# S5 input products of a token pair summed in one PSUM bank, with the first half copied out midway, under a new order of work

## Chip, cores and metric

The kernel runs on one core of one Trainium2 chip. The metric is the device time of one execution in microseconds; three runs of the kernel before give a median of 349.37 us (349.33 to 352.1). Inputs are bfloat16, with 2048 tokens of 640 channels. TensorE (PE) multiplies 128x128 tiles into PSUM, which has 8 banks of 512 float32 columns here; ScalarE (ACT) and VectorE (DVE) copy from PSUM to SBUF and do the element-wise work; GpSimd (POOL) does little; SyncE (SP) issues most of the DMA.

## What is computed

Two kinds of layers alternate twice: x = x + A(LN(x)), x = x + B(LN(x)), and again with the same weights. A is a diagonal complex state space model (S5), B a gated long convolution (H3). Cut to what matters here:

```python
def _A_ref(x, Lambda_re, Lambda_im, B_re, B_im, C_re, C_im, log_dt, Dskip):
    Lam_bar = jnp.exp(dt * Lam)
    B_bar = ((Lam_bar - 1.0) / Lam)[:, None] * Bmat
    Bu = jnp.einsum("bld,pd->blp", x + 0j, B_bar)
    for t in range(L):
        h = Lam_bar[None, :] * h + Bu[:, t, :]
        hs.append(h)
    y = 2.0 * jnp.einsum("blp,dp->bld", hseq, Cmat).real + x * Dskip[None, None, :]

x = x + _A_ref(_layernorm(x, axis=-1), ...)
x = x + _B_ref(_layernorm(x, axis=-1), ...)
x = x + _A_ref(_layernorm(x, axis=-1), ...)
x = x + _B_ref(_layernorm(x, axis=-1), ...)
```

The gate and the filter of B do not depend on x, so the kernel computes the convolution once and uses it in both B layers.

## The kernel before

**Tasks in a written order.** The kernel is a list of 909 named tasks, each on one engine. The string `ORDER` names them in the order in which they are emitted, so each engine runs its own tasks in that order; a suffix `/a`, `/d` or `/p` puts a task that could run on two engines on ACT, DVE or POOL. All SBUF data lies in one tile `arena` and all PSUM data in one tile `banks`; the table `PLACE` gives each buffer its offset in the arena and each PSUM buffer its first bank. Two buffers may share a place at different times, and semaphores then make the later one wait. `Sched.run` does nothing but walk the order.

**The tasks of the set-up and of the convolution.** `yt_*` make Fourier tables, `kv_*` the shifted and gated k and v, `a_*` the S5 weights in four forms (`BT0`, `BT1` for the input, `W0`, `W1` for the output) and the turning table. `yq0` to `yq4` are five blocks of 128 channels of the convolution: products `KA`, `KB`, `VA`, `VB`, `IB`, `IA` on PE, each group `:m` with its copy from PSUM `:e` on ACT or DVE (`evac`, L254 for ACT and L256 for DVE), a pointwise product `_pw` on DVE (L1175 to L1178), a transposition `_tt` and a store `_st` by DMA. Almost all of this is done in the first 160 us.

**The S5 layers.** `A1` and `A2` each run over four chunks `c0` to `c3` of 512 tokens (`ALayer.chunk`). Tokens are taken in pairs, an earlier and a later one, so a chunk has 256 pairs, and the recurrence runs over pairs with the square of the eigenvalue. The steps of a chunk, with their tasks:

- layer norm: statistics `_ln_bn` (first layer, L582 and L583 on DVE) or `_ln_sq` (L555 on ACT), then `_sd`, `_post`, and the normalisation `_id:0` to `:3` on ACT (L609) or DVE (L611);
- `_tu`: a DMA transposition of the normalised chunk, issued by SP (L639);
- the input products in three groups of output blocks j = (0, 1), (2, 3), (4). `_bq` multiplies the second half of `uT` by `BT0` (L658), `_eq` copies the result to the SBUF buffer `q`, `_bp` multiplies the first half of `uT` by `BT1` (L673) and adds `q` by a product with the identity matrix (L675), and `_ev` copies the sum into the buffer `g`. Each j has two parts (real and imaginary) of 256 columns, one bank in all; `_bq` has its banks `pq`, `_bp` its banks `pb`;
- on DVE: `_ri`, a turn of `g` (L690, L691, after a memset L694), `_sc`, the scan (L707), `_cy`, the carry to the next chunk, `_ro`, the turn back, and `_hx`, the subtraction of `q` from the state (L732);
- `_cp:0` to `:3`: the output products with the skip term, 128 tokens each (L755, in the first layer 27 matmuls, of which two add the residual by the identity), and `_xe:0` to `:3`, the copy out (L763 on ACT, L765 or L767 on DVE).

**The B layers.** `B1` and `B2` take the layer norm of the new x (`_ln_*`, `_u`), multiply by the stored convolution (`_mm`, L812) and add (`_m`, L818 and L820). The convolution is loaded from DRAM by `B1l*` and `B2l*`, the output stored by `_st`.

**What the change touches.** The loop over the three groups in `ALayer.chunk`, `ORDER` and `PLACE`. Weights, layer norm, turns, scan, output products, B layers and convolution keep their code.

Of the kernel before, what the change touches and what calls it, by code (L numbers as in the profile page):

```python
# [54 lines left out]
    warm yt_io6 kv_kd a_ldB1 a_pl kv_pd1/p kv_pd3/p kv_pd2/p yt_io0 yt_ph6 yt_f0 kv_dsl yt_ph0 yt_sin6 a_ldB0 yt_io12 kv_pd0/p yt_f2 yq0_kl yt_ph12  # L55
    yt_sin0 a_p0 kv_d0 a_b01:3 kv_k0 kv_lk0 a_b00:2 a_b0e1:3/d kv_k1 a_b00:3 a_b0e0:2/d kv_d1 yt_f3 a_b0e0:3/a kv_k2 a_p1 yt_f4 a_b00:4 yt_sin12 a_p2
    a_b01:2 kv_lv0 yt_neg6 a_ti a_b01:4 yt_h0 yq0_ka a_b0e1:2/d kv_d2 a_b0e1:4/d yq0_KA:m2 kv_ds0 yq0_KA:m3 a_b0e0:4/a yq0_KA:e2/d yq0_KA:m1 a_p3 yq1_kl
    yq0_KA:m0 kv_ds1 yt_neg12 kv_mm0:0 yt_neg0 yq0_KA:e1/a yq0_KA:e0/d kv_ds2 yq0_KA:e3/a a_p4a kv_lv1 a_p4 a_b00:1 a_p5a yq0_KB:m1 a_b0e0:1/a kv_ds3
    kv_ev0:0 a_ta kv_mm0:1 yq0_KB:e1/d kv_ds4 yq0_KB:m4 kv_lk1 a_b00:0 yq1_ka kv_ev0:1 a_p5b yq0_KB:m0 yt_h1 a_b0e0:0/d yq0_KB:m2 yq0_vl yq0_KB:e4/a a_t0
    yq0_KB:e0/a a_b01:0 a_b01:1 yq0_KB:e2/a a_b0e1:1/a a_p6 a_ldC0 a_t1 a_b0e1:0/d kv_mm1:1 a_lamd kv_mm1:0 a_ldC1 kv_ev1:1 a_b10:1 kv_ev1:0 yq0_VA:m2  # L60
    yq0_KB:m3 a_b1e0:1/d yt_Si yq0_VA:m3 yq0_VA:e2/a yq0_KB:e3/d yq1_KA:m1 yq0_VA:e3/a yq0_VA:m0 yq1_KA:e1/d a_b11:4 yq0_VA:e0/a yq0_VA:m1 yq1_KA:m2
    a_b1e1:4/a yq0_VA:e1/d a_b10:4 yt_Ci yq1_KA:e2/a yq1_KA:m3 yq0_VB:m3 a_b1e0:4/a yq1_KA:e3/d yt_h2 yq0_VB:m0 yq0_VB:e3/a yt_h3/p yq1_KA:m0 a_b10:0
    yq0_VB:e0/d yq1_KA:e0/a yq0_VB:m1 yq1_vl a_f a_b1e0:0/a a_ct1 yq0_VB:e1/a yq0_VB:m2 yt_nsi a_wc01:0 a_b11:0 kv_lk2 yq0_VB:m4 a_wm01:0 a_b1e1:0/a
    yq0_VB:e2/d a_wc01:1 a_b11:3 yq0_VB:e4/a xl0 a_wm01:1 a_b1e1:3/a yq1_KB:m2 yq0_pw yq1_KB:m3 yq1_KB:e2/a yq1_KB:m0 kv_lv2 yq1_KB:e3/a yq1_KB:m1
    yq1_KB:e0/a a_b10:2 a_b11:1 yq1_KB:e1/a a_b11:2 kv_lk3 a_b1e1:1/a a_b10:3 a_b1e1:2/a yq1_VA:m3 kv_pd4/p a_b1e0:3/a kv_mm2:1 yq1_VA:e3/a kv_lv3
    yq1_VA:m0 a_b1e0:2/a kv_ev2:1 yq0_IB:m3 yq1_VA:e0/a yq0_IB:m0 yq0_IB:e3/d kv_mm2:0 yq0_IB:e0/a yq2_kl yq1_VA:m2 yq0_IB:m1 kv_ev2:0 yq1_VA:e2/a
    yq0_IB:m4 yq0_IB:e1/a A1c0_ln_bn:2/d yq1_VA:m1 yq2_vl a_ct0 yq1_VA:e1/a yq0_IB:e4/d yq0_IB:m2 A1c0_ln_bn:0/d a_wc00:0 yq1_VB:m0 a_t2 yq1_KB:m4
    a_wm00:0 yq1_VB:e0/a yq0_IB:e2/d a_wc00:1 yq1_VB:m1 yq1_KB:e4/a A1c0_ln_bn:3/a a_wm00:1 yq0_tt kv_mm3:0 yq1_VB:e1/d a_ct4 kv_ev3:0 a_ct2 a_wc04:0
    a_wc02:0 a_wm04:0 yq1_VB:m3 a_wm02:0 a_wc04:1 a_wc02:1 a_wm04:1 yq1_VB:e3/a a_wm02:1 yq1_VB:m2 yq2_ka kv_lv4 yq2_KA:m3 yq2_KA:m0 yq1_VB:e2/d kv_mm3:1
    yq2_KA:e3/a yq2_KA:e0/a yq1_VB:m4 yq2_KA:m2 kv_ev3:1 a_dd yq1_VB:e4/a yq2_KA:e2/a yq2_KA:m1 kv_lk4 yq1_pw yq2_VA:m2 yq2_KA:e1/a yq2_VA:m3 yq2_VA:e2/a  # L70
    xl2 yq2_VA:e3/a yq2_VA:m0 yq2_KB:m0 yq2_VA:e0/a yq2_KB:m2 yq2_KB:e0/a a_ct3 yq2_KB:e2/a yq2_KB:m4 yq3_kl yq0_IA:m0 a_wc03:0 yq2_KB:m1 yq0_IA:e0/a
    a_wm03:0 yq2_KB:e1/a yq1_IB:m3 yq3_vl yq2_KB:e4/d a_wc03:1 A1c0_ln_bn:1/d yq1_IB:m4 kv_mm4:1 yq1_IB:e3/a a_wm03:1 yq1_IB:e4/a yq1_IB:m1 kv_ev4:1
    yq2_VA:m1 yq0_IA:m1 yq1_IB:e1/a yq2_VA:e1/d yq4_kl yq1_IB:m2 yq1_IB:m0 yq0_IA:e1/d yq1_IB:e2/a yq2_VB:m1 yq1_IB:e0/d A1c0_ln_sd kv_mm4:0 yq3_ka
    yq2_VB:e1/d yq1_tt yq2_VB:m0 kv_ev4:0 yq2_KB:m3 yq2_VB:e0/a yq2_VB:m2 A1c0_ln_post yq2_KB:e3/a A1c2_ln_bn:1/d yq2_VB:m3 yq2_VB:e2/a A1c0_id:3/d
    yq2_VB:m4 yq3_KA:m1 A1c0_id:2/d yq2_VB:e3/a yq2_VB:e4/d yq3_KA:m2 A1c0_id:0/d yq3_KA:m3 yq3_KA:e1/a A1c0_id:1/d yq3_KA:m0 yq2_pw A1c0_tu yq3_KA:e2/a
    yq3_VA:m2 yq3_KA:e3/a yq3_KA:e0/a yq1_IA:m0 yq3_VA:e2/a yq3_KB:m4 yq0_st yq1_IA:m1 yq1_IA:e0/a yq3_KB:m1 yq1_IA:e1/a yq3_KB:m3 xl1 yq3_KB:e1/a
    yq3_VA:m3 A1c0_bq:2 yq3_KB:e4/a yq3_KB:e3/a yq3_VA:e3/d yq2_IB:m2 yq1_st A1c0_eq:2/a A1c2_ln_bn:3/d yq2_IB:m4 yq2_IB:m3 yq2_IB:e2/a yq2_IB:e4/d
    yq2_IB:m1 A1c2_ln_bn:2/d yq2_IB:e3/a yq4_vl yq3_VA:m1 yq3_KB:m0 A1c1_ln_bn:2/d yq2_IB:e1/a yq2_IB:m0 yq3_VA:e1/a A1c1_ln_bn:1/d yq3_KB:m2 yq2_IB:e0/a
    A1c2_ln_bn:0/d A1c0_bp:2 yq3_KB:e2/a yq2_tt A1c1_ln_bn:3/d A1c2_ln_sd yq3_VA:m0 A1c0_bq:1 A1c0_ev:2/a A1c2_ln_post yq3_KB:e0/a A1c2_id:3/d yq4_ka
    A1c1_ln_bn:0/d yq3_VA:e0/a yq4_KA:m3 A1c2_id:1/d yq4_KA:m0 A1c0_eq:1/a yq3_VB:m2 yq4_KA:e3/d yq4_KA:e0/a yq3_VB:m1 A1c2_id:2/d A1c2_id:0/d A1c1_ln_sd  # L80
    yq3_VB:e2/a yq3_VB:m3 A1c2_tu yq3_VB:e1/d yq3_VB:m0 A1c1_ln_post yq3_VB:m4 A1c0_bp:1 yq3_VB:e0/a A1c1_id:2/d A1c1_id:0/d yq3_VB:e4/d yq3_VB:e3/a
    A1c1_id:3/d xl3 A1c1_id:1/a yq3_pw yq4_KA:m1 A1c0_bq:0 A1c0_ev:1/a A1c1_tu yq4_KA:e1/a yq4_KA:m2 A1c2_bq:2 A1c0_eq:0/a yq2_IA:m1 A1c0_bp:0 yq2_IA:e1/a
    yq4_KA:e2/a A1c2_eq:2/d yq2_IA:m0 A1c0_xr A1c0_ev:0/a yq3_IB:m1 yq2_IA:e0/a A1c2_bp:2 A1c0_ri yq3_IB:e1/a A1c1_bq:0 A1c2_ev:2/a yq4_KB:m2 yq3_IB:m3
    A1c0_sc yq4_KB:e2/a yq3_IB:m2 yq3_IB:e3/a yq4_KB:m3 A1c1_eq:0/a A1c1_bq:1 yq3_IB:e2/a yq4_KB:e3/a yq3_IB:m4 yq4_KB:m1 A1c1_eq:1/a yq3_IB:e4/d
    yq3_IB:m0 A1c3_ln_bn:1/a yq4_KB:e1/d A1c1_bq:2 A1c3_ln_bn:3/d A1c2_bq:0 yq3_IB:e0/a A1c0_cy A1c0_ro A1c1_eq:2/a yq3_tt yq4_KB:m4 yq4_KB:m0 A1c2_eq:0/a
    A1c1_bp:0 yq4_KB:e0/a yq4_KB:e4/d A1c1_bp:2 A1c3_ln_bn:2/d A1c1_ev:0/a yq4_VA:m2 yq4_VA:m0 yq2_st A1c1_ev:2/d A1c1_bp:1 yq4_VA:e0/a A1c3_ln_bn:0/d
    yq4_VA:e2/a yq4_VA:m1 yq4_VA:m3 A1c1_ev:1/d A1c2_bp:0 yq4_VA:e1/a A1c1_ri yq4_VA:e3/a A1c2_bq:1 A1c2_ev:0/a A1c3_ln_sd yq4_VB:m3 A1c2_eq:1/a A1c0_hx
    yq4_VB:m2 yq4_VB:e3/a yq3_IA:m1 A1c3_ln_post yq4_VB:m4 yq4_VB:e2/d A1c2_bp:1 yq3_IA:e1/a A1c1_sc yq4_VB:e4/a yq4_VB:m1 yq4_VB:m0 yq4_VB:e1/a A1c0_cp:3
    yq4_VB:e0/a A1c2_ev:1/a a_w10:3 A1c0_xe:3/d a_w11:0 a_w1e0:3/a a_w10:4 yq4_pw a_w1e1:0/a a_w10:1 a_w1e0:4/a a_w11:2 a_w1e0:1/a a_w10:0 a_w1e1:2/a
    a_w11:3 a_w10:2 A1c0_cp:1 a_w1e0:2/a a_w1e0:0/a a_w1e1:3/a a_w11:4 A1c0_xe:1/a yq3_IA:m0 A1c1_cy A1c1_xr a_w11:1 a_w1e1:4/a A1c1_ro yq4_IB:m1  # L90
    a_w1e1:1/a yq4_IB:m3 A1c3_id:3/a yq3_IA:e0/a A1c0_cp:0 yq4_IB:e1/a yq3_st yq4_IB:e3/a A1c1_hx yq4_IB:m2 A1c3_id:1/d A1c0_xe:0/a A1c3_id:2/d yq4_IB:m0
    A1c3_id:0/a yq4_IB:e2/d yq4_IB:m4 A1c0_cp:2 yq4_IB:e0/a A1c2_ri yq4_IB:e4/a yq4_tt A1c1_cp:3 A1c0_xe:2/a B1c0_ln_nm B1c0_ln_sq:1 A1c2_sc B1c0_ln_sq:0
    B1c0_ln_sq:3 A1c1_cp:0 A1c3_tu A1c1_xe:3/a yq4_IA:m1 A1c1_xe:0/a yq4_IA:m0 A1c2_xr A1c1_cp:2 A1c2_cy yq4_IA:e0/a yq4_IA:e1/d B1c0_ln_sq:2 yq4_st
    B1c0_ln_sd B1c0_ln_post A1c2_ro A1c1_cp:1 A1c1_xe:2/a B1c0_u:2/a A1c3_bq:1 B1l0 A1c1_xe:1/a B1c0_u:0/d B1c1_ln_nm B1c1_ln_sq:2 A1c2_hx A1c3_bq:0
    B1c1_ln_sq:3 B1l1 A1c3_eq:1/d B1c1_ln_sq:1 B1c0_u:3/d B1c1_ln_sq:0 A1c3_xr A1c2_cp:0 B1c0_u:1/d B1c0_mm B1c1_ln_sd A1c3_eq:0/a B2l0 B1c0_m:2
    B1c1_ln_post B1c0_m:0 B1c1_u:0/a A1c3_bq:2 B1c1_u:1/d A1c2_xe:0/a B1c0_m:1 A1c3_bp:1 B1c1_u:3/a B1c0_m:3 A1c3_eq:2/a B1c1_u:2/d A2c0_ln_nm
    A2c0_ln_sq:0 B1c1_mm A1c3_bp:2 A2c0_ln_sq:3 B1c1_m:1 A2c0_ln_sq:2 A1c3_bp:0 B1c1_m:2 A2c0_ln_sq:1 B1c1_m:0 A2c0_ln_sd A1c3_ev:1/a A2c0_ln_post
    A1c2_cp:1 A2c0_id:1/d A1c3_ev:2/a A2c0_id:2/d A1c3_ev:0/a B1c1_m:3 A2c0_id:0/a A1c3_ri A2c0_id:3/a A1c2_cp:3 A2c1_ln_nm A2c1_ln_sq:0 A2c0_tu
    A1c2_xe:1/a A2c1_ln_sq:1 A2c1_ln_sq:3 A1c2_cp:2 A1c3_sc B1l2 A2c1_ln_sq:2 A2c1_ln_sd A1c2_xe:3/a A2c0_bq:0 A1c2_xe:2/a B1c2_ln_nm B1c2_ln_sq:1
# [514 lines left out]
class ALayer:  # L614
# [6 lines left out]
    def chunk(self, c, src, sums_in, x_ready, resid, s_x, sums_out, s_src, reload):  # L621
# [26 lines left out]
        for gi, js in enumerate(((0, 1), (2, 3), (4,))):  # L648
# [3 lines left out]
            def e_bq(_, js=js, s_pq=s_pq):  # L652
                pq = s_pq.get().rearrange("p (j c n) -> p j c n", c=2, n=NB)
                uT, bt0 = s_uT.get(), w["BT0"].get()
                for jj, j in enumerate(js):
                    for c2 in range(2):
                        for k in range(NJ):
                            nc.tensor.matmul(pq[:, jj, c2, :], lhsT=bt0[:, c2, k, j * P:(j + 1) * P],  # L658
                                             rhs=uT[:, 2:4, k, :], start=(k == 0), stop=(k == NJ - 1))
# [721 lines left out]
```

## Time and profile before

| What | Value |
|---|---|
| Median of three runs | 349.37 us |
| Profiled execution, first to last instruction | 348.2 us |
| Granted TensorE clock, mean over the span | 0.977 |
| DVE: last instruction ends | 345.0 us |
| PE: last matmul ends | 331.7 us |
| Copy of 128x1024 from PSUM: ACT, DVE | 1.033 us, 1.220 us |
| Copy of 128x640 from PSUM: ACT, DVE | 0.720 us, 0.816 us |
| Copy of 128x512 from PSUM: ACT, DVE | 0.603 us, 0.689 us |
| Normalisation of 128x640: ACT; DVE from float32, from bfloat16 | 0.911 us; 0.608, 0.434 us |
| Turn on DVE: products, sum | 2.844 us, 1.504 us |
| Scan on DVE, one of two parts | 2.833 us |

The profile is one execution. Busy time of an engine is the time in which at least one of its instructions runs. Matmuls are pipelined: a row's mean duration of a matmul is its whole way through the array, and several are under way at once, so a busy PE is not a PE at its peak; the distance between the starts of two matmuls in a row is what one costs. An idle time is put down to what ended it. In the windows, the first number pair is the stretch of the span and its length, and after each engine's busy time stands the number of its instructions.

### The profile page before, as it was taken

To read this page: it belongs to the slowest core of one execution; us is meant where nothing else is said; L and a number is where in the kernel's file an instruction comes from. 1 tells how busy PE (TensorE), PEld (TensorE's weight loads), DVE (VectorE), ACT (ScalarE), POOL (GpSimd) and SP (SyncE) were. 2 spreads that over 40 slices of the span, in tenths; PEclk is the share of its full clock that TensorE was granted. 3 is DMA by queue.
4 is the path that set the end of the run, shared out by engine and by line. 5 is a ranking of instruction groups with operands and counts; after the bars stand their busy time and mean duration, and the time that the engine had idled before them with its cause. 6 is when DMAs were issued, how large, how long until landed. Compare 5 with 4: busy or idle time off the path is not lost.

```text
span 348.2 us, 9466 instructions
## 1 busy us (share of the span) xinstructions
PE 310.0 (89%) x4110; PEld 248.4 (71%) x4110; DVE 326.5 (94%) x449; ACT 256.3 (74%) x411; POOL 20.6 (6%) x62
## 2 busy tenths in 40 slices
PE   7777897779799999999999999999999999998910
PEld 7665887768698899896666786876877787654500
DVE  8999898899999989798999999999999999999996
ACT  6999898797998768566867689897776856008850
POOL 5690000010000000000000000000000000000000
PEclk9999999899999999999999999999999999999975
DMA  8999999887999920800259642315009500000024
GB/s 231 218 170 257 186 228 154 167 185 152 180 230 179 218 77 10 174 2 0 77 120 215 189 177 52 100 18 130 6 5 227 135 15 2 0 2 0 3 112 188
DMA packets 105868, 41.71 MB, mean 120 GB/s; under 512 B 98141, under 2 KB 100706, under 8 KB 105826
## 3 DMA queue, kind: packets, MB, share of 16 engines
q1 hardware_dynamic: 105680, 41.10, 53.7%
q8 instruction: 32, 0.52, 0.6%
q14 instruction: 10, 0.08, 0.1%
q10 hardware_dynamic: 146, 0.01, 0.0%
HBM read 19.02 MB, written 5.24 MB: 70 GB/s over the span
## 4 chain that ended last, share of the span: by engine, by line
PE 62%; DVE 27%; ACT 6%; issue 3%; POOL 0%; DVEq 0%; ACTq 0%; POOLq 0%
PE banks L755 18%; PE banks L658 11%; PE banks L673 11%; ACT arena L254 5%; DVE arena L256 3%; DVE arena L690 3%; DVE arena L707 3%; DVE arena L820 3%; DVE arena L767 3%; PE banks L1197 2%; PE banks L1198 2%; PE banks L675 2%; PE banks L1098 2%; PE banks L1289 2%; PE banks L1122 2%
## 5 line engine op out<-in xcount | busy, mean ns | idle before, releaser
L254 ACT ACTIVATE arena<-banks 128x1024 bf16<-128x1024 f32 (+4 forms) x150 | 129.5, 929 | 31.9 <-PE banks L658 9.2
L755 PE MATMUL banks<-arena 128*128 128x128 bf16 (+1 forms) x800 | 101.0, 283 | 1.7 <-DVE arena L767 1.7
L755 PEld LDWEIGHTS <-arena 128*128 128x128 bf16 x800 | 60.6, 98 | 41.7 <-issue 1.9
L673 PE MATMUL banks<-arena 128*128 128x256 bf16 x400 | 53.2, 273 | 0.0
L256 DVE CAST arena<-banks 128x1024 bf16<-128x1024 f32 (+4 forms) x43 | 41.7, 979 | 5.6 <-PE banks L675 2.5
L658 PE MATMUL banks<-arena 128*128 128x256 bf16 x400 | 46.2, 273 | 0.0
L690 DVE TENSOR_TENSOR arena<-arena 128x5160 bf16<-128x5160 bf16 x16 | 45.5, 2844 | 0.4
L707 DVE TENSOR_TENSOR_SCAN arena<-arena 128x1290 bf16<-128x1290 f32 x16 | 44.7, 2833 | 0.3
L673 PEld LDWEIGHTS <-arena 128*128 128x128 bf16 x400 | 38.6, 98 | 4.6
L658 PEld LDWEIGHTS <-arena 128*128 128x128 bf16 x400 | 38.5, 98 | 4.7
L555 ACT ACTIVATE junk<-arena,nmean 128x640 bf16<-128x640 f32 x48 | 39.7, 827 | 1.3
L1122 PE MATMUL banks<-arena 128*128 128x128 bf16 x170 | 35.5, 221 | 4.6 <-DVE arena L427 1.5
L1125 PE MATMUL banks<-arena 128*128 128x128 bf16 x170 | 35.7, 221 | 0.0
L1127 PE MATMUL banks<-arena 128*128 128x128 bf16 x150 | 33.2, 221 | 0.0
L1124 PE MATMUL banks<-arena 128*128 128x128 bf16 x150 | 33.2, 221 | 0.0
L609 ACT ACTIVATE arena<-arena,nmr,rstd 128x640 bf16<-128x640 f32 (+1 forms) x32 | 27.8, 912 | 5.8 <-DVE nmr L568 3.8
L691 DVE TENSOR_TENSOR arena<-arena 128x2580 bf16<-128x2580 bf16 x16 | 24.1, 1504 | 0.5
L675 PE MATMUL banks<-arena,ident_bf 128*128 128x256 bf16 x80 | 21.8, 273 | 0.0
L763 ACT ACTIVATE arena<-banks 128x640 f32<-128x640 f32 x15 | 10.4, 697 | 14.0 <-PE banks L755 14.0
L1197 PE MATMUL banks<-arena 128*128 128x128 bf16 x160 | 19.6, 219 | 0.7 <-ACT arena L254 0.5
L1198 PE MATMUL banks<-arena 128*128 128x128 bf16 x160 | 19.4, 219 | 0.3 <-DVE arena L1178 0.3
L1124 PEld LDWEIGHTS <-arena 128*128 128x128 bf16 x150 | 14.8, 99 | 5.1 <-issue 5.1
(196 smaller groups left out, 498.8 us busy)
## 6 DMA issues: line engine op xcount, KB each, us to landing
arena<-in_A_x_dram SPq DMA_DIRECT2D x8, 640.0 KB, 5.5
arena<-ysd SPq DMA_DIRECT2D x8, 640.0 KB, 5.9
arena<-in_B_ssm_k_dram SPq DMA_DIRECT2D x5, 512.0 KB, 7.7
arena<-in_B_v_dram SPq DMA_DIRECT2D x5, 512.0 KB, 6.3
ysd<-arena SPq DMA_DIRECT2D x5, 512.0 KB, 4.5
out_dram<-arena SPq DMA_DIRECT2D x8, 320.0 KB, 2.2
arena<-in_A_B_im_dram SPq DMA_DIRECT2D x1, 800.0 KB, 5.2
arena<-in_A_B_re_dram SPq DMA_DIRECT2D x1, 800.0 KB, 7.1
```

The lines of the kernel that those rows point to most:

```text
L254: nc.scalar.activation(out, in_, ACT.Copy)
L256: nc.vector.tensor_copy(out, in_)
L555: nc.scalar.activation(small.junk, src(q), ACT.Square, bias=st["nmean"][:, i:i + 1], scale=1.0, accum_out=st["ssq"][:, i:i + 1])
L658: nc.tensor.matmul(pq[:, jj, c2, :], lhsT=bt0[:, c2, k, j * P:(j + 1) * P], rhs=uT[:, 2:4, k, :], start=(k == 0), stop=(k == NJ - 1))
L673: nc.tensor.matmul(pb[:, jj, c2, :], lhsT=bt1[:, c2, j, k, :], rhs=uT[:, 0:2, k, :], start=(k == 0), stop=False)
L690: nc.vector.tensor_tensor(tt, gs[:, :, None].to_broadcast([P, 2, 2, n]), by_pairs(w["tab"].get().rearrange("p i j b -> p (i j b)"), n), AL ...
L707: nc.vector.tensor_tensor_scan(gv, rt, gv, 0.0, ALU.mult, ALU.add)
L755: nc.tensor.matmul(pc[:, o0:o1], lhsT=lh, rhs=rh, start=(n == 0), stop=(n == len(ops) - 1))
L1122: nc.tensor.matmul(ps[:, g, 0, :], lhsT=T["Cf"].get()[:, q, :], rhs=are, start=True, stop=single)
L1124: nc.tensor.matmul(ps[:, g, 0, :], lhsT=T["Sf"].get()[:, q, :], rhs=A[:, 2 * q + 1, :], start=False, stop=True)
L1125: nc.tensor.matmul(ps[:, g, 1, :], lhsT=T["NSf"].get()[:, q, :], rhs=are, start=True, stop=single)
L1127: nc.tensor.matmul(ps[:, g, 1, :], lhsT=T["Cf"].get()[:, q, :], rhs=A[:, 2 * q + 1, :], start=False, stop=True)
```

## The change

In each of the three groups the second product now adds into the bank of the first one. `_bq` starts the bank once (its very first matmul), `_eq` copies the bank's state out to `q`, and `_bp` then goes on adding into the same bank, without a start and without identity matmuls. `_ev` copies the sum. So `pq` is gone and `_bp` has 20 instead of 24 matmuls in a group of two blocks, 10 instead of 12 in the last. `q` is still needed by `_hx`. `skip_group_check` tells the language's checker that the group is read before its end.

```diff
-            s_pq, s_pb = S.bank(f"{nm}_pq{gi}", len(js)), S.bank(f"{nm}_pb{gi}", len(js))
-            n = len(js)
+            s_pb, n = S.bank(f"{nm}_pb{gi}", len(js)), len(js)
 
-            def e_bq(_, js=js, s_pq=s_pq):
-                pq = s_pq.get().rearrange("p (j c n) -> p j c n", c=2, n=NB)
+            def e_bq(_, js=js, s_pb=s_pb):
+                pb = s_pb.get().rearrange("p (j c n) -> p j c n", c=2, n=NB)
...
-                            nc.tensor.matmul(pq[:, jj, c2, :], lhsT=bt0[:, c2, k, j * P:(j + 1) * P],
-                                             rhs=uT[:, 2:4, k, :], start=(k == 0), stop=(k == NJ - 1))
+                            nc.tensor.matmul(pb[:, jj, c2, :], lhsT=bt0[:, c2, k, j * P:(j + 1) * P],
+                                             rhs=uT[:, 2:4, k, :], start=(c2 == k == 0), stop=(c2 == 1 and k == NJ - 1), skip_group_check=True)
...
                             nc.tensor.matmul(pb[:, jj, c2, :], lhsT=bt1[:, c2, j, k, :],
-                                             rhs=uT[:, 0:2, k, :], start=(k == 0), stop=False)
-                        nc.tensor.matmul(pb[:, jj, c2, :], lhsT=ident[:], rhs=s_q.get()[:, c2, j, :], start=False, stop=True)
+                                             rhs=uT[:, 0:2, k, :], start=False, stop=(c2 == 1 and k == NJ - 1), skip_group_check=True)
```

`ORDER` and `PLACE` are new from end to end. The 909 tasks are the same, in another order. 93 change their engine: 45 go from ACT to DVE, 43 from DVE to ACT, and five small ones from POOL to DVE. A part of the new order, around the first chunk's input products:

```
yq1_IA:e0/a A1c0_bq:2 yq3_KB:e2/a yq3_VA:m1 yq2_IB:m2 yq3_VA:e1/d yq1_st A1c0_eq:2/a
yq2_IB:m0 yq4_vl yq2_IB:e2/a A1c1_ln_bn:1/d yq2_IB:m1 yq2_IB:e0/a A1c1_ln_bn:0/d yq2_IB:e1/a yq2_IB:m3 yq4_KA:m2
yq0_st yq2_IB:e3/a a_dd yq4_KA:e2/d yq2_IB:m4 A1c0_bp:2 yq2_IB:e4/a yq3_VA:m2 yq3_VA:e2/d yq3_VA:m0 A1c0_bq:1 yq2_tt
yq3_VA:e0/a A1c2_ln_post A1c2_id:3/d A1c0_ev:2/a yq3_VB:m2 A1c2_id:0/d A1c0_eq:1/a A1c2_id:2/d A1c2_id:1/d yq3_VB:m4
yq3_VB:m3 A1c1_ln_bn:3/d yq3_VB:e4/a A1c1_ln_sd A1c0_bp:1 yq3_VB:e2/d A1c2_tu yq3_VB:e3/d A1c1_ln_post A1c1_id:0/d
A1c0_ev:1/a yq4_KA:m1 A1c1_id:1/d yq3_VB:m1 yq4_KA:e1/d yq3_VB:m0 A1c0_bq:0 yq3_VB:e1/a yq3_VB:e0/a A1c1_id:2/d
A1c1_id:3/d A1c1_tu yq3_pw A1c2_bq:2 A1c0_eq:0/a yq2_IA:m1 A1c0_bp:0 A1c2_eq:2/a yq2_IA:e1/a A1c2_bp:2 A1c0_ev:0/a
```

## The prediction

> **What bounds the kernel now.** I read the busy shares first, then the stretches of the span, then the chain that ended last, then the rows of the work that the change removes or moves. From the page:
>
> ```profile
> span 348.2 us, 9466 instructions
> ...
> PE 310.0 (89%) x4110; PEld 248.4 (71%) x4110; DVE 326.5 (94%) x449; ACT 256.3 (74%) x411; POOL 20.6 (6%) x62
> ...
> L673 PE MATMUL banks<-arena 128*128 128x256 bf16 x400 | 53.2, 273 | 0.0
> ...
> L658 PE MATMUL banks<-arena 128*128 128x256 bf16 x400 | 46.2, 273 | 0.0
> ...
> L675 PE MATMUL banks<-arena,ident_bf 128*128 128x256 bf16 x80 | 21.8, 273 | 0.0
> ```
>
> VectorE (DVE) is busy 94% of the whole span and TensorE 89%; neither says which one a stage waits for. The stretches do (columns: length, then busy time and count for PE, weight loads, DVE, ACT, POOL, then clock and DMA):
>
> ```profile
> 0.00:96.00 96.00, 76.05 (x1730) 68.95 (x1731) 88.74 (x149) 84.20 (x118) 20.60 (x62) 0.98 1.00 194
> 96.00:168.00 72.00, 71.93 (x913) 62.02 (x912) 65.45 (x85) 54.64 (x71) 0.00 (x0) 1.00 0.50 107
> 168.00:312.00 144.00, 143.77 (x1319) 106.48 (x1318) 139.57 (x166) 96.66 (x180) 0.00 (x0) 1.00 0.35 89
> 312.00:348.00 36.00, 18.29 (x150) 10.91 (x149) 32.77 (x52) 20.81 (x45) 0.00 (x0) 0.83 0.19 73
> ```
>
> From 96 to 312 us PE has no idle time, while DVE has 6.5 us in the first 72 and 4.4 in the next 144. Before 96 DVE has 7.3 and PE is loose; after 312 DVE is alone (3.2 idle, nearly all after its last instruction ends at 345.0, while the last store lands). So PE leads from 96 to 312, but with DVE 97% busy close behind. The chain shows what a product really takes, and DVE's order of time where it waits:
>
> ```profile
> 125.83 2.18 PE banks L658 x20
> ...
> 159.06 3.27 PE banks L755 x27
> ```
>
> ```profile
> 143.76 0.69 DVE L256 CAST arena<-banks 128x512 bf16<-128x512 f32 x1 [0.59 <-PE banks L675]
> ...
> 146.97 1.23 DVE L256 CAST arena<-banks 128x1024 bf16<-128x1024 f32 x1 [1.48 <-PE banks L675]
> ```
>
> Twenty products of 256 columns pass in 2.18 us: 109 ns each, not the 273 of the row, which holds the pipeline's length. And DVE's two waits end on the identity product L675 itself.
>
> **The change, part by part.** *Identity products.* Each of 8 chunks loses 10, 80 in all: 80 x 109 ns = 8.7 us of PE time, 1.1 per chunk. Three chunks do these products before 168 us (3.3 us), five after (5.4). The other 800 products stay.
>
> [...]
>
> *The new wait.* The second input product (`bp`) adds into the bank that the copy `eq` reads, so its first matmul waits for the whole copy. Before, only an identity product did, five matmuls (0.55 us) later. PE runs in order: all queued behind `bp` waits too, and with it the copies on ACT and DVE. The copy needs 0.16 us from the last matmul's slot to its end (273 less 109), then 0.03 (product ended 118.55, copy began 118.58 in the first chunk), then 1.03 on ACT: 1.2 us. The new order leaves, between the two products of a group, other PE work of at least 1.5 us (chunk A1c0, group 0), 2.0 twice, 2.2 five times, more elsewhere. With ACT free no group stalls. But ACT took up some copies late in this trace: 2.8 us (A1c1, group 0), 2.7 (A2c0, group 2), 3.1 (A2c2, group 1). With that lateness and the new covers of 2.46, 2.18 and 3.27 the stalls are 1.5, 1.3 and 1.1. Bounds: 0 to 3.9 us of PE. I take 1.5 before 168, and let the rest lie in PE's new slack.
>
> [...]
>
> *Copies moved between engines.* 45 go from ACT to DVE, 43 back, 5 small ones from POOL to DVE. By rows: 1024-wide copies (1.22 us on DVE) 19 to and 21 from DVE, -2.4; 640-wide (0.82) net 7 to DVE, +5.7; 512- and 256-wide one less each, -1.1; normalisations -2 x 0.61 and +1 x 0.43, -0.8; POOL's five +0.5. Sum +1.9 us. Durations overlap on DVE: its 449 add up to 348.4 where 326.5 are busy, 49 ns each; seven more take 0.3 off, so +1.5. ACT gets 1.4 less; its 92 idle us hide that.
>
> *New order and places.* Before 96 us everything is reshuffled and nothing removed. (Below, "summed" means: the durations of this trace's rows, or PE's slots of 216, 109, 56 and 29 ns, added along an engine's order in the program text.) POOL makes its longer iota (1.26 us) ahead of the one that ACT's first sine needs (0.81); ACT's table load until 4.66 hides most of that. The first chunk's transposition is issued after 95.3 us of summed DVE durations instead of 99.0, but has 1.6 us more PE work ahead of its first product. Value 0; bounds from the slices of 24 us: DVE idle was 3.3 in the worst of them and 0.6 in the best, so -2 to +4. On SP two loads of the last layer come behind the first output store; they land in 5.9 us and DVE has 13 us of other work queued before the user: nothing. After DVE's last turn its work is the same to 0.1 us.
>
> *What DVE gets back.* In 96 to 168 it waits 1.25 (for ACT's copy behind L675), 0.59, 1.48 and 0.88 us on PE: 4.2. PE saves 3.3 less 1.5, and at chunk A1c1's turn the new order needs 116.2 us of summed PE work against 119.3, with DVE at 145.4 against 146.0: PE is 2.5 us further ahead. I take 3.0 back; bounds 0 and 5. In 168 to 312 PE gets ever further ahead (at A2c3's turn DVE's sum leads PE's by 41.8 instead of 29.2), so DVE alone is the bound; of its 4.4 idle the fed slices keep about 0.5 per 24 us, 3.0. I take 1.4; bounds 0 and 3.4. What is late next is DVE itself.
>
> Sum, against the profiled span: 348.2 + 1.5 - 3.0 - 1.4 = 345.3. The median 349.37 stands 1.1 above the span: **346.4 us**, 0.85% faster.
>
> **Rivals.** *PE's whole saving counts.* For: PE is without idle for 216 us. Against: DVE's idle there is 11.0, part of it short handovers. 349.4 - 8.7 + 1.5 = 342.2.
>
> *The change does not bring its gain at all:* the removed PE time lies beside DVE work. For: DVE 97% busy from 168 on. Against: the four waits named. 349.4 + 1.5 = 350.9.
>
> *Slower, by the order of the first 120 us.* There DVE and ACT both feed PE's banks, and each late copy holds the next product. Price: if every 24 us there lost what the worst slice (48 to 72) did, 3.3 x 5 = 16.5 against 8.9 now, +7.6: 346.4 + 7.6 = 354.0. It decides from 6.5 us on. Against: the same work went through with 0.6 idle in the next slice.
>
> *Slower, by the new wait* in A1c0 to A1c2, where PE binds. If ACT were 2.8 us late for every group there, covers of 1.55, 2.02, 2.46, 2.64, 2.02, 2.64 and 3.97 would leave stalls of 2.4 + 2.0 + 1.5 + 1.4 + 2.0 + 0.9 + 0.2 = 10.4, less the 3.3 saved: +7.1, and 349.4 + 1.5 + 7.1 - 1.4 = 356.6. From 3.3 us of stalls the stage gains nothing. Against: seven of the nine copies there began within 1 us of their product in this trace.
>
> **Chances and range.** Forecast 0.47 (its own range 344 to 349), full saving 0.18, no gain 0.18, early order 0.11, new wait 0.06. A measurement tells about 1% (3.5 us) from no change: below 345.9 is faster. Of the forecast's 0.47 some 0.20 lie below it, with 0.18 of the full saving 0.38 faster; 0.27 and 0.17 make 0.44 within; the slower two and the edge of no gain 0.18. The range 342 to 352 leaves out 0.08 below and 0.12 above; its ends also cover the bounds -2 and +4 of the early order around 346.4.
>
> **What would show it.** No row with the identity in the input products; PE busy about 301 us (8.7 less, as it is saturated there); DVE busy 328.0; DVE idle in the 72 us after the first input product down to about 3.5. Wrong if PE shows gaps before `bp` rows released by ACT's copy of more than 2 us in all before A1c2's turn, if DVE's idle before 96 us is off 7.3 by over 2, or if PE has no idle before A2c3's turn.

## The result, and the profile after

The changed kernel takes 362.89 us (median of 4 runs, 362.08 to 364.09) against 349.69 us (4 runs, 349.33 to 352.1). The medians differ by 13.2 us; the ratio of the runs on record is 1.0356, 95% interval 1.0316 to 1.0397, which is 12.5 us of 350, and runs are compared by that ratio below. In e10 two of the four runs were over 1.5% slower than its fastest one, and they are left out. The forecast of 346.4 us was wrong, and so was its range.

The head of the page of the changed kernel, its busy shares, the rows of the two input products and its granted clock by fortieths of the span (line numbers are 27 to 29 higher than before, so L658 is now L686 and L673 is L701):

```profile
span 361.2 us, 9307 instructions
...
PE 310.3 (86%) x4030; PEld 246.9 (68%) x4030; DVE 329.8 (91%) x456; ACT 256.5 (71%) x409; POOL 18.3 (5%) x57
...
PEclk9887899959989999999999999999999999999965
...
L686 PE MATMUL banks<-arena 128*128 128x256 bf16 x400 | 46.0, 273 | 4.5 <-DMA arena<-arena 4.5
...
L701 PE MATMUL banks<-arena 128*128 128x256 bf16 x400 | 46.1, 273 | 0.0
```

The identity row is gone, as it should be. The second product (L701) never waits: its last column is 0.0, where the prediction had put 1.5 us. The first one (L686) waits 4.5 us in four places for a chunk's transposition, where it waited 0.0 before. The stretches say where the time went (columns as before):

```profile
0.00:96.00 96.00, 76.22 (x1546) 69.34 (x1548) 82.96 (x159) 78.65 (x105) 18.28 (x57) 0.88 0.98 185
96.00:168.00 72.00, 66.90 (x1000) 59.60 (x993) 62.25 (x66) 50.16 (x61) 0.00 (x0) 0.98 0.62 128
168.00:312.00 144.00, 138.68 (x1259) 100.74 (x1258) 139.21 (x170) 103.92 (x197) 0.00 (x0) 1.00 0.33 80
```

Before 96 us DVE now idles 13.0 us (96 less 82.96) instead of 7.3, at a granted clock of 0.88 instead of 0.98. In the next 72 us it idles 9.8 instead of 6.5, and PE has gaps. From 168 to 312 us little has changed (4.8 against 4.4). Followed by tasks, the pointwise product of the first block (`yq0_pw`) starts at 48.6 us instead of 43.2, that of the third (`yq2_pw`) at 103.9 instead of 91.7, and the first S5 product at 110.3 instead of 98.3. This is `yq2_pw` before; the line of the changed kernel stands further below:

```profile
91.73 2.42 DVE L1175 TENSOR_TENSOR arena<-arena 128x4352 bf16<-128x4352 bf16 x1
```

So the code that was changed first runs 12 us later. By then DVE has idled for 15.9 us instead of 7.3; the other 3.4 us are DVE work that the new order puts ahead of it. DVE's last instruction ends 13.0 us later (345.0 to 358.0): 9.7 us more idle time, 3.3 more busy time.

Four of the new waits, in the timelines of ACT, of DVE and of PE (start, length, instruction, and in brackets the idle time ahead of it and what ended it):

```profile
76.11 2.86 ACT L283 ACTIVATE arena<-banks 128x1024 bf16<-128x1024 f32 x3 [4.14 <-DMA arena<-arena]
```

```profile
75.30 1.23 DVE L1095 TENSOR_TENSOR arena<-banks,arena 128x1024 bf16<-128x1024 f32 x1 [1.27 <-PE banks L1089]
78.87 0.42 DVE L285 CAST arena<-banks 128x256 bf16<-128x256 f32 x1 [2.35 <-PE banks L1154]
...
103.91 2.42 DVE L1202 TENSOR_TENSOR arena<-arena 128x4352 bf16<-128x4352 bf16 x1 [2.64 <-DMA arena<-arena]
```

```profile
28.50 0.22 PE L1151 MATMUL banks<-arena 128*128 128x128 bf16 x1
32.00 0.29 PE L1152 MATMUL banks<-arena 128*128 128x128 bf16 x1 [3.27 <-issue]
```

ACT stands 4.1 us ahead of `yq2_KA:e0`: it writes buffer `yq2_AK`, which the new table puts at place 3020, where `yq0_T` lies, and SyncE's transposition `yq0_tt` still reads that until 76.0. Meanwhile its banks stay full, PE waits, and DVE waits for PE (1.27 and 2.35). In the same way `yq2_pw` writes `yq2_Z` at 1648, the place of `yq1_T`, and waits 2.6 us for the transposition `yq1_tt`. Before, neither ACT nor DVE waits for a transposition anywhere (waits of 0.2 us or more). The third kind is PE's 3.3 us in the middle of one product, ended by nothing that the profile shows ("issue").

### The profile page after: what moved, and what is told of

It reads as the page before. It is cut to its first block, busy times and chain, and to the rows that moved or that the text cites. A ratio compares the mean times of both kernels' runs of the same rounds, so it can differ in the third digit from the quotient of the medians.

```text
span 361.2 us, 9307 instructions
## 1 busy us (share of the span) xinstructions
PE 310.3 (86%) x4030; PEld 246.9 (68%) x4030; DVE 329.8 (91%) x456; ACT 256.5 (71%) x409; POOL 18.3 (5%) x57
## 5 line engine op out<-in xcount | busy, mean ns | idle before, releaser
L283 ACT ACTIVATE arena<-banks 128x1024 bf16<-128x1024 f32 (+4 forms) x152 | 131.4, 928 | 49.5 <-PE banks L701 17.8
L782 PEld LDWEIGHTS <-arena 128*128 128x128 bf16 x800 | 60.6, 98 | 42.8 <-DVE arena L718 1.4
L686 PE MATMUL banks<-arena 128*128 128x256 bf16 x400 | 46.0, 273 | 4.5 <-DMA arena<-arena 4.5
L285 DVE CAST arena<-banks 128x1024 bf16<-128x1024 f32 (+4 forms) x41 | 39.2, 978 | 11.2 <-PE banks L1154 4.7
L701 PE MATMUL banks<-arena 128*128 128x256 bf16 x400 | 46.1, 273 | 0.0
L686 PEld LDWEIGHTS <-arena 128*128 128x128 bf16 x400 | 38.3, 98 | 9.9 <-DMA arena<-arena 4.4
L638 ACT ACTIVATE arena<-arena,nmr,rstd 128x640 bf16<-128x640 f32 (+1 forms) x33 | 29.0, 915 | 18.8 <-DVE nmr L597 18.8
L701 PEld LDWEIGHTS <-arena 128*128 128x128 bf16 x400 | 38.7, 98 | 4.4
L1152 PE MATMUL banks<-arena 128*128 128x128 bf16 x170 | 36.9, 227 | 3.3 <-issue 3.3
L1149 PE MATMUL banks<-arena 128*128 128x128 bf16 x170 | 36.4, 226 | 1.9 <-ACT arena L283 1.6
L1154 PE MATMUL banks<-arena 128*128 128x128 bf16 x150 | 33.8, 225 | 0.0
L1151 PE MATMUL banks<-arena 128*128 128x128 bf16 x150 | 33.8, 225 | 0.0
L1224 PE MATMUL banks<-arena 128*128 128x128 bf16 x160 | 19.7, 219 | 1.0 <-ACT arena L283 0.7
L1152 PEld LDWEIGHTS <-arena 128*128 128x128 bf16 x170 | 17.3, 102 | 3.9 <-issue 3.8
L1225 PE MATMUL banks<-arena 128*128 128x128 bf16 x160 | 19.5, 219 | 0.0
L1125 PEld LDWEIGHTS <-arena 64*128 64x128 bf16 x320 | 11.9, 108 | 9.5 <-issue 8.0
```

Of the source, the lines that this page charges most:

```text
L283: nc.scalar.activation(out, in_, ACT.Copy)
L285: nc.vector.tensor_copy(out, in_)
L686: nc.tensor.matmul(pb[:, jj, c2, :], lhsT=bt0[:, c2, k, j * P:(j + 1) * P], rhs=uT[:, 2:4, k, :], start=(c2 == k == 0), stop=(c2 == 1 and ...
L701: nc.tensor.matmul(pb[:, jj, c2, :], lhsT=bt1[:, c2, j, k, :], rhs=uT[:, 0:2, k, :], start=False, stop=(c2 == 1 and k == NJ - 1), skip_gro ...
L782: nc.tensor.matmul(pc[:, o0:o1], lhsT=lh, rhs=rh, start=(n == 0), stop=(n == len(ops) - 1))
L1149: nc.tensor.matmul(ps[:, g, 0, :], lhsT=T["Cf"].get()[:, q, :], rhs=are, start=True, stop=single)
```

## The experiments

Theory: the new order, engines and places of the first 100 us make the loss; the new code alone costs nothing. Rivals: the code costs (the second product behind the copy); the work behind 100 us costs; one single wait, or the places, make all of it; the lower clock makes it. "Old" is the kernel before, "new" the changed one. Ratios are to runs of the old kernel on the same chip, with 95% intervals.

**Code and order apart.** `e1_code_old_order` is the new code in the old order:

```diff
 yq3_IB:m0 A1c3_ln_bn:1/a yq4_KB:e1/d A1c1_bq:2 A1c3_ln_bn:3/d
-A1c2_bq:0
 yq3_IB:e0/a A1c0_cy A1c0_ro A1c1_eq:2/a yq3_tt yq4_KB:m4 yq4_KB:m0
...
 yq4_VA:m2 yq4_VA:m0 yq2_st A1c1_ev:2/d
+A1c2_bq:0
```

> The new code (one bank for both products, no identity products) in the order of the kernel before. Engines, places in the arena and the order of all tasks are as before, except that one product (A1c2 bq:0) and its copy come some 15 tasks later and 20 PSUM buffers get another bank, because a bank is now held longer. Theory 1 (the loss comes from the new order of the first 100 us, the code alone costs nothing): 346 to 350 us, nearest 348.5, and DVE idle before 96 us stays near 7.3. Rival 1 (the code alone costs: products of the second half now stand behind the copy): 356 us or more, with PE gaps ahead of the second products. Rival 2 (the clock alone): as theory 1 here.

Measured: 349.31 us, 0.9972 (0.9952 to 0.9993). Its page:

```profile
span 347.5 us, 9307 instructions
...
PE 303.6 (87%) x4030; PEld 241.0 (69%) x4030; DVE 326.2 (94%) x449; ACT 256.1 (74%) x411; POOL 20.6 (6%) x62
```

In the old order the code alone gains about 1 us: PE's busy time falls by 6.4 us (310.0 to 303.6) and DVE's does not move. Rival 1 is out.

`e2_old_code_new_order` puts the identity products back into the changed kernel, each pair of buffers in one bank:

```diff
-    "A1c0_pb0": 4,
+    "A1c0_pq0": 4, "A1c0_pb0": 4,
...
+                        nc.tensor.matmul(pb[:, jj, c2, :], lhsT=ident[:], rhs=s_q.get()[:, c2, j, :], start=False, stop=True)
```

> The order, engines and places of the changed kernel with the old code: identity products are back; the second product still has the bank of the first, so it still waits for the copy. Theory 1 (order of the first 100 us): 361 to 366 us, nearest 363.5, as 80 identity products (8.7 us of TensorE) mostly lie beside DVE's work. Rival 1 (the code costs): the time falls by half of the loss or more, 357 or less. Third case (the removed products do pay, and their gain is hidden in the loss): 367 or more.

Measured: 366.1 us, 1.0434 (1.0395 to 1.0472). That is 0.1 us above the theory's range and 0.9 below the third case. Against 1.0356 the removed products are worth 0.8%, 2.7 us, in the new order (by the intervals 0.2 to 1.3%): the order makes the loss with the old code too, and the gain is real though small.

**The orders cut in two.** Kernels of new code whose first tasks stand in one order and the rest in the other, with every buffer born behind the cut placed anew:

```diff
-ORDER = new
+ORDER = old[:k] + [t for t in new if t not in old[:k]]
```

The first two, cut at the first S5 input product (in e4 old and new change places):

> The new code; tasks up to the first S5 input product (about 98 us) in the order, engines and places of the kernel before, all later tasks in the order and engines of the changed kernel (places packed anew). Theory 1 (the loss arises before 98 us): 346 to 352 us, nearest 348.5. Rival 3 (the order after 98 us, or the merged bank, costs): 357 or more.

> The mirror: the new code; tasks up to the first S5 input product in the order, engines and places of the changed kernel, all later tasks in the order and engines of the kernel before (places packed anew). Theory 1: 359 to 365 us, nearest 362. Rival 3: 353 or less.

Measured: e3 371.34 us, 1.0611 (1.0564 to 1.0657); e4 366.2 us, 1.0454 (1.0396 to 1.0512). In e3 the first product starts at 98.1 us, as in the old kernel, but then DVE waits 4.2 us for a load that had come late at the cut, and 5.0 for a transposition that reads the place which it is to write. e4 has a wait of that kind on DVE at 137 us, 5.1 us long, beside two that the changed kernel has too (2.4 and 1.9 us). Neither decides: the way I made them added waits. Four more cuts, placed with more care up to the second layer, had it again:

> New code; the first 101 tasks (to about 26 us) in the order, engines and places of the kernel before, the rest in the order and engines of the changed kernel, places packed anew without a buffer that is written soon after a transposition reads its place. Where the two orders are cut, the sets of tasks done differ by four. Theory (the loss adds up from local order and TensorE's stalls between 26 and 100 us): 358 to 361 us, since only the 2 us of the start come back. Rival C (the start sets everything behind it): 353 or less.

> As the run before with the first 203 tasks (to about 50 us) of the kernel before; the sets at the cut differ by five tasks. Theory: yq0_pw starts at 43 to 44 us, the 3.4 us gap of TensorE at 28.5 us and the half clock behind it are gone, 354 to 357 us: the 5.4 us that yq0_pw was late come back. Rival D (the loss is made in 50 to 100 us; the early part only eats slack): 359 or more.

> As the run before with the first 261 tasks (to about 72 us) of the kernel before. Theory: 351 to 354 us, with yq1_pw at 71 us. Rival D: 356 or more.

> As the run before with the first 428 tasks (to about 122 us) of the kernel before; the sets at the cut differ by two tasks. Theory: 348 to 351 us, all of the loss is back. Rival E (the order, engines or banks behind 122 us cost as much): 356 or more.

| Run | Time, ratio | Largest waits of DVE or ACT on a transposition or store |
|---|---|---|
| e9 | 370.62 us, 1.0610 (1.0545 to 1.0676) | 6.3 (DVE), 1.7 (DVE) |
| e10 | 365.91 us (two runs), 1.0451 (1.0355 to 1.0546) | 4.5 (ACT), 2.6 (ACT) |
| e11 | 363.68 us, 1.0385 (1.0343 to 1.0427) | 4.1 (DVE) |
| e12 | 362.10 us, 1.0343 (1.0298 to 1.0388) | 6.8 (DVE) |

All four missed. In e9 the cut itself also held PE for 5.7 us at 26 us. The last told more. DVE's timeline in e12, ahead of the turn of chunk A2c1:

```profile
268.74 0.07 DVE L725 MEMSET arena<- 128x10 uint32 x1
270.60 3.01 SPq L672 DMA_TRANSPOSE arena<-arena  x1
275.59 2.85 DVE L721 TENSOR_TENSOR arena<-arena 128x5160 bf16<-128x5160 bf16 x1 [6.78 <-DMA arena<-arena]
```

My table had put the turn's buffer `A2c1_t` where `A2c2_u` lay, three tasks after the transposition of `A2c2_u` was issued. `e16_old_order_to_122_clean` has the order and engines of e12, and such clashes taken out by another table of places:

```diff
 ORDER = old[:428] + [t for t in new if t not in old[:428]]
-    "A2c1_t": 2309,
+    "A2c1_t": 373,
...
```

> As the run with the first 428 tasks of the kernel before, places packed anew once more: that run had put A2c1_t into a place from which A2c2_u was being transposed, and DVE waited 6.8 us for it at 269 us. Theory (the loss lies before 122 us, but DVE's additional 2.7 us of work come partly later): 350 to 354 us. Rival E: 357 or more.

Measured: 354.72 us, 1.0100 (1.0059 to 1.0142), 7.4 us below e12 by the medians, 8.5 by the ratios. Two things follow. Places alone, with nothing else changed, can cost more than half of what this change lost. And with the old order up to 122 us, 9.0 of the 12.5 us are back, not all: by the ratios e16 is still 4.5 us above e1. Its page:

```profile
span 352.3 us, 9295 instructions
...
PE 303.3 (86%) x4009; PEld 240.9 (68%) x4030; DVE 328.1 (93%) x448; ACT 258.0 (73%) x416; POOL 20.6 (6%) x62
```

(21 records of matmuls are missing there.) DVE is busy 1.9 us longer than in e1 and idles 2.9 us more up to its last instruction, so the new order, engines and PSUM banks behind 122 us cost too.

**Single waits taken away.** Each edit leaves the rest of the changed kernel alone:

```diff
 e6:
- yq0_KA:m3 kv_ds0 yt_Si yq0_KA:e1/d
...
- yq0_KB:m1 yt_Ci yq0_KB:m0
...
- yq0_KB:e0/d yq0_vl a_b01:1
+ yq0_KB:e0/d yq0_vl yt_Si yt_Ci a_b01:1
 e7:
- yq1_VB:m1 A1c2_ln_bn:1/d a_ct2
...
- yq1_IB:m3 A1c2_ln_bn:2/d
+ yq1_IB:m3 A1c2_ln_bn:1/d A1c2_ln_bn:2/d
 e13:
- a_lamd kv_mm1:0 yq0_KB:m3 kv_ev1:0
...
- yq0_KB:e3/d a_b11:4
+ yq0_KB:e3/d kv_mm1:0 kv_ev1:0 a_b11:4
 e5, e8:
-    "yq2_AK": 3020, "yq2_Z": 1648,
+    "yq2_AK": 2059, "yq2_Z": 1843,
```

> The changed kernel, order untouched, with 18 buffers of the first 100 us at other places in the arena, so that yq2_AK no longer lies where yq0_T is still being transposed, nor yq2_Z where yq1_T is. Theory A (these two shared places hold ACT 4.1 us at 72 us and DVE 2.6 us at 101 us, and with them DVE's waits of 1.3 and 2.4 us at 74 and 76): 5 to 7 us off, 356 to 358 us; no wait of ACT or DVE on a transposition at 72 and at 101. Rival (those waits only show a lateness that lies elsewhere, in the queue of SyncE or in TensorE): under 2 us off, 361 or more.

> The changed kernel with the two table transpositions yt_Si and yt_Ci put behind the load yq0_vl in the order, as in the kernel before; nothing else moves. Theory B (the transpositions ahead on SyncE hold yq0_vl from about 23 to 31.5 us, and the DMA that they make holds TensorE's instructions, with the gap of 3.4 us at 28.5): yq0_VA starts 5 us earlier, the gap at 28.5 us shrinks to under 1.5 us, yq0_pw starts 3 to 5 us earlier, the time is 358 to 361 us. Rival (what is lost there is not on the path, DVE has other work): under 1 us off.

> The changed kernel with one DVE task, the statistics A1c2 ln_bn:1, some 40 tasks later, beside ln_bn:2 of the same chunk. It waits 2.5 us at 65 us for its load. Theory: DVE gets those 2.5 us back if nothing else is late there, 360 to 361 us. Rival (DVE would only wait later, for TensorE and ACT at 74 to 79 us): under 1 us off.

> The three edits together: the 18 other places, the table transpositions behind yq0_vl, the statistics later. If the three account for the loss: 349 to 353 us. If they share one cover (DVE's and TensorE's own work is what is longer in the new order): 356 or more.

> The changed kernel with one product of the set-up (kv_mm1:0, 64 matmuls of 64 columns) and its copy put four tasks later, behind yq0_KB:m3 and its copy; one PSUM buffer gets another bank. Theory F (TensorE used up its instructions: kv_mm1 in two rows takes 256 of them in 2.5 us, and the next 16 KB fetch takes 4.6 us while the DMA engines are full): yq0_KB:m3 runs without the 3.4 us gap, its copy ends 3 us earlier, a shorter gap shows at the moved product, 360 to 362 us. Rival (the gap belongs to yq0_KB:m3's own operands): the gap stays at yq0_KB:m3. If the time stays at 362.9 although the gap goes, this gap is not on the path.

Measured: e5 363.52 us, 1.0395 (1.0333 to 1.0456); e6 361.27, 1.0336 (1.0281 to 1.0390); e7 362.61, 1.0347 (1.0291 to 1.0404); e8 363.45, 1.0373 (1.0325 to 1.0421); e13 362.59, 1.0330 (1.0279 to 1.0381). None differs from 1.0356 by more than the intervals leave open. e5 and e8 had a new clash: `yq1_y` came to lie where `A1c0_u` was read and `A1c0_q` is written, and ACT waited 3.0 and 3.5 us in e5 (2.7 and 3.5 in e8) for it. e7's edit removed its wait, and the profiled execution ends only 0.8 us earlier. e6 and e13 hold a pair. In e6 the load `yq0_vl` (a transposition by DMA) is issued at 22.6 instead of 31.5 us, but the gap in `yq0_KB:m3` stays (2.8 us) and PE comes to `yq0_VA` only at 36.3 (37.1 in the changed kernel). In e13 that product runs without its gap, at 27.2 to 28.2 us; PE's waits from 24 to 46 us there (line waited for, us in total, times, longest):

```profile
PE banks L1093 <- DVE arena L289: 2.2, 1, 2.2
PE banks L1129 <- DMA arena<-arena: 1.3, 1, 1.3
```

The moved product now waits 2.2 us for its bank, and `yq0_VA` (L1129) waits until the late load lands, at 37.9 us. Two limits stand there side by side, so neither edit alone brings its 3 us. Both together were not run.

`e15_three_edits_clean` repeats e8 with all places packed anew:

```diff
-    "yq1_y": 3068, "wr01": 1012, "kv1": 3078,
+    "yq1_y": 2948, "wr01": 2192, "kv1": 2168,
```

> As the run with the three edits together, with all places packed anew so that no buffer is written soon after a transposition that still reads its place (that run had put yq1_y into such a place, with new waits of ACT of 2.7 us at 99 and 3.5 us at 110 us). Theory A (shared places, the late load and the tables' transpositions make the loss of 26 to 110 us): 354 to 358 us. Rival (each wait taken away shows again at the next late step): 361 or more.

Measured: 370.34 us, 1.0573 (1.0515 to 1.0631). ACT's timeline says that I had made one more:

```profile
50.38 0.79 ACT L455 ACTIVATE arena<-banks,s_F 128x640 f32<-128x640 f32 x1 [5.15 <-DMA arena<-arena]
```

`kv1` reaches from 2168 to 2231, and `a_wc01:0` writes `wr01` there, 29 tasks after `yq1_vl` began to read that place: 29 tasks are far in `ORDER`, and 5 us short in time.

**Places by times, and engines.** So `e17_new_order_clean_places` has its places chosen by the times of the changed kernel's own trace; order, engines and banks are the changed kernel's:

```diff
 ORDER = new
-PLACE = new
+PLACE = new, 110 of 188 buffers moved, each to a place free 0.3 us or more before its first write
```

> The changed kernel: order, engines and banks untouched, 110 of 188 buffers at other places in the arena, chosen by the times of the changed kernel's trace so that no engine and no DMA issue has to wait for the former user of a place (the three waits on transpositions of ACT at 72 us, 4.1 us, and of DVE at 101 and 119 us, 2.6 and 1.0 us, and SyncE's waits on former users are among them). Theory A (places make half or more of the loss): 354 to 358 us, yq2_pw at 99 us or earlier. Rival (order and engines make it, the waits on places only show where it is late): 360 us or more.

Measured: 360.61 us (6 runs), 1.0281 (1.0241 to 1.0322). Two stretches, of the changed kernel, then of e17, then of e1 for the old order:

```profile
0.00:48.00 48.00, 37.22 (x694) 33.54 (x695) 41.72 (x101) 39.05 (x58) 18.28 (x57) 0.86 1.15 225
48.00:96.00 48.00, 39.00 (x856) 35.80 (x855) 41.24 (x59) 39.60 (x49) 0.00 (x0) 0.89 0.82 144
```

```profile
0.00:48.00 48.00, 36.88 (x690) 33.31 (x691) 41.39 (x101) 38.78 (x57) 18.19 (x57) 0.86 1.13 224
48.00:96.00 48.00, 40.38 (x973) 36.62 (x971) 43.96 (x65) 42.19 (x53) 0.00 (x0) 0.96 0.79 154
```

```profile
0.00:48.00 48.00, 37.20 (x776) 34.19 (x777) 44.59 (x90) 43.01 (x64) 18.79 (x57) 1.00 1.10 218
48.00:96.00 48.00, 38.99 (x961) 34.85 (x959) 44.27 (x60) 41.46 (x56) 1.83 (x5) 0.96 0.91 171
```

Between 48 and 96 us DVE gets 2.7 us back (43.96 less 41.24) and the clock rises from 0.89 to 0.96; `yq2_pw` starts 5.2 us earlier. The first 48 us stay as slow as they were: DVE idles 6.6 us there, in e1 3.4. So the places cost 0.75%, 2.6 us, of the median: real, but far from half.

`e14_new_order_old_engines` keeps the new order and places and puts all 93 tasks back on their old engines:

```diff
- yq0_KA:e2/a yq0_KA:e1/d yq0_KA:e0/a
+ yq0_KA:e2/d yq0_KA:e1/a yq0_KA:e0/d
...
```

> The changed kernel, order, places and banks untouched, with all 93 tasks back on the engine that they had in the kernel before. Theory (45 tasks to DVE and 43 from it cost DVE 2.7 us of summed durations): 359 to 361 us. Rival (the engines were chosen for this order, and another choice makes copies late): 363 or more.

Measured: 397.59 us, 1.1322 (1.1269 to 1.1375), with DVE busy 327.7 us (2.1 less) and idle for 66. The rival is right by far: each engine works in the given order, and with another division of the copies the same order makes them late (DVE's longest wait there is 7.0 us, for a second input product).

`e18_old_order_clean_places` does with e1 what e17 does with the changed kernel:

```diff
 ORDER = as in e1
-PLACE = as in e1
+PLACE = as in e1, 119 of 188 buffers moved by the times of e1's trace
```

> The new code in the order of the kernel before (as the first run of this study, 349.3 us), with 119 of 188 buffers at other places by the same method, from that run's own trace. If waits on places cost there too, 346 to 348.5 us, a version that is faster than both kernels. If that order was free of such waits on its path, 348.5 to 350. If the loads that now start earlier take DMA from others, 351 or more.

Measured: 349.31 us (12 runs), 0.9968 (0.9943 to 0.9992): the same as e1. So the old order had no such wait on its path. e1 and e18 are 0.3% faster than the kernel before (both intervals end just below 1).

## Why the prediction was wrong, point by point

**The failed step** is "New order and places", with "Before 96 us everything is reshuffled and nothing removed" and "Value 0; bounds [...] -2 to +4". Equal sums along an engine's order were taken for equal time, and the term cost 13.4 us. (PE's slots in those sums are distances between starts in the trace of the kernel before: 216 ns for 512 columns and 56 for 128 at L755, 109 for 256 at L658, 29 for 64 at L1225.) Set side by side, the runs part the 12.5 us (3.56% of 350) like this: the code -1.0 (e1), order, engines and PSUM banks behind 122 us +4.5 (e16 less e1), the same up to 122 us +6.3 (e17 less e16), places +2.6 (changed kernel less e17). Each part is uncertain by up to 2 us, and that they add up is assumed. The sum of an engine's work says nothing of who waits for whom: of DVE's 13.0 us, 9.7 are waits. The bounds failed too: they came from the old kernel's own slices, that is, from an order without these waits.

**What was to be read.** The two clashes of places can be seen in the diff of `PLACE`: `yq0_T` and `yq2_AK` both at 3020, `yq1_T` and `yq2_Z` both at 1648, with a transposition reading the first and 25 and 32 tasks from its issue to the write of the second. The description of the kernel names the rule ("semaphores then make the later one wait"), and the prediction did not go through the table. Yet that reading alone would have given about a fifth of the loss.

**The identity products.** 8.7 us of PE time were predicted; in e1 PE's busy time falls by 6.4, and in the changed kernel, part of which ran at half clock, not at all (310.0 to 310.3). Their worth in time, 4.4 us in the sum (the 3.0 and 1.4 that DVE was to get back), is 1.0 in the old order and 2.7 in the new one: right in sign, a quarter to six tenths in size. The two measurements do not differ by more than their intervals.

**What DVE gets back** (3.0 and 1.4) came only in part. In e1 DVE idles 7.4 us from 96 to 168 us (72 less 64.64 busy) instead of 6.5, and 3.4 from 168 to 312 instead of 4.4. The four waits on L675 are gone, but others stand in the first stretch. The longest comes close to where two of the four stood (143.8 and 147.0 us before) and ends on the second product itself, while PE has no gap of more than 0.2 us there:

```profile
148.42 1.23 DVE L289 CAST arena<-banks 128x1024 bf16<-128x1024 f32 x1 [2.49 <-PE banks L705]
```

**The new wait**, put at 1.5 us, is 0.0 on L701 in the changed kernel and 0.4 us on the same line of e1. The other PE work between the two products covered it, as the prediction's covers of 1.5 us and more said; no stall by a late ACT shows on L701.

**Copies moved between engines.** Summed by rows +1.9 was predicted and +2.7 is measured (349.65 to 352.33; the prediction's 348.4 for the first sum is 1.25 too low by the trace); in busy time +3.3 instead of +1.5. Of the miss of 1.8 us, 0.8 lies in the sum, and 1.0 in the overlap of neighbouring durations, which shrank where it had been expected to grow.

**The rivals.** "Slower, by the order of the first 120 us" named the right place at a chance of 0.11. Its price, 7.6 us from the worst slice of the old kernel, was short: DVE's idle time there went from 8.9 to 18.8 us. Its mechanism, late copies that hold PE's banks, is only one of those seen, beside shared places, a late load and PE's gap. The rival by the new wait is refuted (0.0 us on L701). For the code by itself, the rival without any gain came nearest, with 1.0 us measured against 0; the one with PE's whole saving of 8.7 us is refuted. The prediction's own test ("if DVE's idle before 96 us is off 7.3 by over 2") points at the right stretch, with 13.0.

**Open.** What in the order makes the 6.3 us before 122 us is not settled. In e17 `yq0_pw` is 5.6 us late already, and the next three blocks' `_pw` are late by 5.2, 7.0 and 7.2 us, so most of the lateness stands by 48 us. The late load and PE's gap at 28.5 us stand there in parallel, and `yq0_KA` starts 1.5 us later (14.4 against 12.9 us in the kernel before). What the half clock costs by itself was not tried. The 51 runs of the old kernel beside the experiments give a hint: 15 with a mean granted clock under 0.97 (mean 0.965) have a median of 351.15 us, 33 with 0.974 or more (mean 0.976) one of 350.24. Carried on to the changed kernel's 0.94, that is some 3 us, an estimate; the runs do not tell whether a wait of PE lowers the clock or follows from it, so this is not shown.

## What to carry to other kernels

When a change brings a new order of all the work, the operations that it removes are the smaller half: go through the new order for who waits for whom, and take its bounds from what that order could do, not from how smoothly the old one ran. In a table of shared places look first for buffers whose last reader is a transposition or a store, and count the distance to the next writer in microseconds, since 29 tasks were 5 us too few. And to see what a piece of code is worth, run it once in the order that is known to be good.

## What the hardware showed beyond that

**PE seems to run out of instructions.** The 3.3 us gap at 28.5 us lies between two matmuls of one accumulation, with no wait. It stands at the same product in nine of the twenty profiled runs, 2.8 to 4.4 us long; in the other eleven none of PE's waits that end on "issue" is over 1.0 us. The trace's transfers of kind "instruction" on the queue that keeps step with PE (q8) are 16 KB each, 31 in all, and one comes per 255 of PE's instructions (matmuls and weight loads) in the mean. In the undisturbed part (130 to 200 us) one comes per 244 to 278; here 402 had passed since the last one when the next began, at 29.64 us. It took 1.03 us, and PE went on 1.3 us after its end. That count alone is no mark (in e13, 391 passed without a gap at 22 us). Counted from the start at the mean of 255 to a transfer, PE stood 451 instructions ahead when this transfer began, and never more than 364 at the start of another one in this trace, nor more than 425 in the kernel before, which has no such gap. The two products ahead of the gap are 128 matmuls of 64 columns, and 256 instructions in about 2.5 us. The 4.6 us of e13's expectation fit the stretch from 26.0 us, where the last 256 instructions ahead of the gap begin, to the end of the transfer at 30.67; the transfer itself is the 1.03 us. In e13, with half of those matmuls moved behind, the gap was gone from this place, so it does not belong to the product's operands; that instructions were what PE lacked fits, and is not shown otherwise. The window from 24 to 36 us has a DMA share of 1.22.

**The clock falls in steps.** The changed kernel's records show half clock from 14.5 to 21.3, 31.6 to 38.4, 72.5 to 82.8 and 103.2 to 106.6 us, 27.3 us in all, against 3.4 us (65.9 to 69.3) before, both without the half clock behind the last matmuls; the last three spells begin during or behind gaps of PE of 1.4 to 3.3 us. Other gaps of 1.4 to 2.0 us (at 128, 195, 291 and 328 us) start none. The spells last 6.83, 6.83, 10.24 and 3.41 us, the one before 3.41: multiples of 3.41 us. The spell at 72.5 us follows gaps of 1.6 and 1.4 us. What starts a spell is not shown.
